# One parametric relu in place of a scaling and a bitwise and in the weights' split, with a new order of the program

## The chip, the cores and the metric

One NeuronCore of a Trainium2 chip runs the kernel. The metric is the device time of one execution in microseconds; three timed runs of the kernel before are shown.

## The reference

Windowed attention over 4 batches of 8 heads (768 positions, 64 values a head), then a feed-forward layer with a softmax-weighted activation on its output, seen as 3072 rows of 512:

```python
# _attn_ref, q, k, v of (4, 8, 768, 64); block 32, window 16
k_sum = k.reshape(B, H, nb, block, D).max(axis=3)
v_sum = v.reshape(B, H, nb, block, D).mean(axis=3)
scores_l = scale * q @ k^T          # kept where |i - j| < 16
scores_s = scale * q @ k_sum^T + log(block)
a = softmax(concat(scores_l masked, scores_s))
attn = a @ concat(v, v_sum)
# _moe_ref, x of (3072, 512), w_in 512 x 1024, w_out 1024 x 512
h = x @ w_in
solu = h * softmax(h)
ln = (solu - mean(solu)) / sqrt(var(solu) + 1e-6) * g_ln
return ln @ w_out
```

q, k, v and g_ln are float32 in memory; w_in and w_out come in as 64-bit floats and are cut into two 32-bit words each.

## The kernel before

The 3072 rows are 24 tiles of 128 rows. For each half of a group of 256 positions (a step, named by batch, group and half as 2_1_0) TensorE computes scores (tile s), VectorE their row maxima (L678), ScalarE the exponentials (L686), VectorE or GpSimd the division by the sum (tile e, L370 on VectorE or L371 on GpSimd), TensorE turns the result (tile t), ScalarE or VectorE copies it out of PSUM (tile at) and TensorE multiplies it by the values (tile x). Then, for each row tile, TensorE computes the first product (tile h; from row tile 8 on for two tiles at a time with seven instead of eight products: hu, hl, hf), the activation runs over ScalarE, VectorE and GpSimd (tile he), he is turned (by TensorE as lt, or from row tile 6 on by VectorE and a way through DRAM) and TensorE computes the second product (tile o), which ScalarE or VectorE scales (os) and a DMA writes out. Each product of 32-bit values is three matmuls: every operand is split into a high and a low part (xh and xl, lh and ll, two halves of w).

The weights arrive as pairs of words (tile raw, the high word in words(1), the low word in words(0)) in 16 pieces of 128 x 512: 8 of w_in (raw_97 to raw_103, raw_108 and raw_109), 8 of w_out (raw_124 to raw_131). `rounded` makes 32-bit floats of each in the tile cv: the high word scaled by 2^-112 (L454 on ScalarE or L456 on VectorE), its sign bit alone (L460, VectorE), the top of the low word (L465 or L467), a shift of the high word by three bits (L470), and the sum of the halves (ADD_W, L370 or L371). Then w's high part is a cast (w_in) or a scaling by g_ln (w_out, L487), and its low part a difference (w_out: L489). The centring of he stands in L1011 and its neighbours, the copies out of PSUM in L363 (ScalarE) and L364 (VectorE), the smaller of hm's two parts in L992.

Nothing is issued in the order in which it is written. Every step is an `op` with an engine, a duration that the planner assumes, the buffers that it reads and writes, and in places other engines with their durations. `Plan.order` lists the operations by these durations; `SEARCHED` is a list of seeds whose random shifts of due times and preferences were kept by a search. The result is one fixed instruction order on each engine. Into TensorE's order `issue` puts dummy matmuls on a zero tile (`idle`, L1300; 80 of them here) wherever the plan has TensorE waiting within its first 80 us. They write to a PSUM tile that is free and belong to no result.

Of the kernel before, what the change touches and what calls it, by code (L numbers as in the profile page):

```python
# [1345 lines left out]
```

## Time and profile before

| | us |
|---|---|
| median of three runs (lowest to highest) | 363.81 (363.76 to 363.94) |
| span of the profiled execution, first to last instruction | 362.6 |
| TensorE busy | 354.2 (98%) |
| VectorE busy | 305.5 (84%) |
| ScalarE busy | 281.6 (78%) |
| GpSimd busy | 157.3 (43%) |

The profiled execution has only its span; the runs' median is 1.2 us longer, which is the time that lies around the first and last instruction. Busy shares are averages over parts with different limits, and the ends of matmuls are modelled: a matmul of 512 columns is shown as some 0.39 us long although the next one starts 0.23 us later, so a wait of TensorE shows as idle only for the part that goes beyond that.

### The profile page before, as it was taken

The numbers are of one execution on the slowest core, as the hardware profiler recorded it, in microseconds if no ns is written. First come the engines' busy times: TensorE is split into PE (matmuls) and PEld (weight loads), VectorE is DVE, ScalarE is ACT, GpSimd is POOL, SyncE is SP. The second block draws the span as 40 slices with busy tenths as digits, with TensorE's granted clock in tenths as the row PEclk, the third lists the DMA queues.
The fourth block names the chain that finished last, engine by engine and source line by source line (L and its number), as shares of the span: only waits on it lengthen the run. The fifth ranks groups of instructions, "written<-read, shape, count | busy, mean of one in ns | idle before, by whom it ended". The sixth has DMA issues, their size and how long they took to land.

```text
span 362.6 us, 9384 instructions
## 1 busy us (share of the span) xinstructions
PE 354.2 (98%) x3332; PEld 277.0 (76%) x3332; DVE 305.5 (84%) x964; ACT 281.6 (78%) x815; POOL 157.3 (43%) x290
## 2 busy tenths in 40 slices
PE   8999999999999998999999999999999999999995
PEld 3537667768777786788788888888888888888885
DVE  4989999998999999997899999797797996947430
ACT  4888999979869978989698696896796796946320
POOL 6612330166968867423924147350335054534200
PEclk9999999999999999999999999999999999999999
DMA  7999994145325435538489384384164283344611
GB/s 241 413 414 405 359 397 155 62 113 165 130 77 196 136 131 173 172 95 273 141 270 285 117 280 153 114 288 148 57 201 174 55 276 101 116 147 168 209 58 58
DMA packets 28530, 68.19 MB, mean 188 GB/s; under 512 B 3852, under 2 KB 13324, under 8 KB 26948
## 3 DMA queue, kind: packets, MB, share of 16 engines
q1 hardware_dynamic: 24620, 60.87, 49.6%
q10 hardware_dynamic: 3864, 6.74, 5.2%
q8 instruction: 26, 0.43, 0.5%
q14 instruction: 20, 0.16, 0.1%
HBM read 49.55 MB, written 15.73 MB: 180 GB/s over the span
## 4 chain that ended last, share of the span: by engine, by line
PE 63%; DVE 22%; DMA 5%; ACT 3%; SPq 3%; issue 2%; POOL 1%; ACTq 0%; DVEq 0%
PE o L1108 29%; PE hu L932 10%; PE hl L932 5%; PE x L761 4%; PE s L659 3%; PE h L913 3%; DVE e L678 3%; PE t L714 3%; DMA qt<-in_q 2%; DMA farl<-tbl 2%; PE hf L932 2%; DVE e L370 2%; SPq L602 2%; DVE w L489 2%; DVE hm L990 2%
## 5 line engine op out<-in xcount | busy, mean ns | idle before, releaser
L1108 PE MATMUL o<-w,lh 128*128 128x512 f32 (+1 forms) x400 | 128.0, 385 | 0.9 <-DVE w L489 0.9
L1108 PEld LDWEIGHTS o<-w,lh 128*128 128x128 f32 x400 | 74.1, 188 | 16.4 <-DVE w L489 1.2
L1108 PE MATMUL o<-w,ll 128*128 128x512 f32 (+1 forms) x200 | 76.2, 381 | 0.0
L686 ACT ACTIVATE e<-e,nm 128x120 f32<-128x120 f32 x192 | 73.2, 388 | 0.0
L913 PE MATMUL h<-w,xh 128*128 128x512 f32 x128 | 43.0, 400 | 0.0
L1108 PEld LDWEIGHTS o<-w,ll 128*128 128x128 f32 x200 | 37.6, 188 | 6.8
L678 DVE CUSTOM_DVE_ANT_0 e<-s,mask 128x120 f32<-128x120 f32 x192 | 40.6, 276 | 0.5 <-PE s L659 0.3
L686 ACT ACTIVATION_READ_ACCUMULATOR e<-e,nm 128x1 f32 x192 | 37.0, 193 | 0.0
L363 ACT COPY at<-t 120x512 f32<-120x512 f32 x43 | 22.9, 591 | 11.0 <-PE t L714 8.6
L913 PEld LDWEIGHTS h<-w,xh 128*128 128x128 f32 x128 | 24.0, 188 | 7.3 <-ACT at L363 0.8
L1015 ACT ACTIVATE he<-he,nmu 128x512 f32<-128x512 f32 x36 | 24.7, 721 | 4.4 <-DVE nmu L1006 4.3
L761 PEld LDWEIGHTS x<-at,vt 120*64 120x64 f32 (+1 forms) x768 | 24.4, 138 | 4.1 <-issue 2.6
L371 POOL TENSOR_TENSOR ll<-lt,lh 128x512 fp32r<-128x512 f32 x11 | 16.5, 1512 | 23.5 <-DVE lh L364 15.8
L1038 DVE STREAM_TRANSPOSE tbl<-he 128x1024 f32<-128x1024 f32 x18 | 22.3, 1239 | 5.3 <-DMA farl<-tbl 2.7
L1114 ACT ACTIVATE os<-o,y 128x512 f32<-128x512 f32 (+1 forms) x20 | 13.5, 675 | 17.0 <-PE o L1108 16.8
L761 PE MATMUL x<-at,vt 120*64 120x64 f32 (+1 forms) x768 | 26.5, 224 | 0.0
L588 POOL TENSOR_TENSOR st_v<-st_v 96x512 f32<-96x512 f32 (+3 forms) x28 | 22.1, 797 | 8.3 <-DMA st_v<-in_vb 7.8
L1018 ACT ACTIVATE sq<-he 128x1024 bf16<-128x1024 f32 x24 | 25.3, 1056 | 0.1
L913 PE MATMUL h<-w,xl 128*128 128x512 f32 x64 | 25.1, 393 | 0.3 <-DVE xl L770 0.3
L363 ACT CAST lh<-lt 128x512 fp32r<-128x512 f32 x33 | 19.2, 608 | 7.8 <-DMA lt<-farl 5.6
L995 ACT ACTIVATE he<-hs,hm 128x512 f32<-128x512 f32 x24 | 17.1, 716 | 8.3 <-DVE hm L985 8.3
L370 DVE TENSOR_TENSOR e<-e,z 128x960 f32<-128x960 f32 x18 | 23.1, 1281 | 0.1
(175 smaller groups left out, 836.0 us busy)
## 6 DMA issues: line engine op xcount, KB each, us to landing
vt<-in_v SPq DMA_DIRECT2D x12, 1024.0 KB
farl<-tbl SPq DMA_DIRECT2D x18, 512.0 KB
lt<-farl SPq DMA_DIRECT2D x72, 128.0 KB
kraw<-in_k SPq DMA_DIRECT2D x16, 400.0 KB
out<-os ACTq DMA_DIRECT2D x23, 256.0 KB
qt<-in_q SPq DMA_DIRECT2D x11, 512.0 KB
raw<-in_w_in SPq DMA_DIRECT2D x8, 512.0 KB
raw<-in_w_out SPq DMA_DIRECT2D x8, 512.0 KB
```

What stands on the lines that cost most here:

```text
L363: by = {act: lambda: nc.scalar.copy(out=to(), in_=of()), dve: lambda: nc.vector.tensor_copy(out=to(), in_=of()), pool: lambda: nc.gpsimd.t ...
L370: by = {dve: lambda: nc.vector.tensor_tensor(out=to(), in0=a(), in1=b(), op=kind), pool: lambda: nc.gpsimd.tensor_tensor(out=to(), in0=a() ...
L588: op(pool, 0.15 + w * 0.0021, lambda w=w, o=o: nc.gpsimd.tensor_tensor(out=o.ap[:n, :w], in0=x.ap[:n, :w], in1=x.ap[:n, w:2 * w], op=ALU.add),
L678: nc.vector.tensor_tensor_reduce(out=e.ap[:, n, :], in0=sc.ap[:, j, (2 * i + up) * KC:(2 * i + up + 1) * KC], in1=mask[:, mi, :], scale=-S ...
L686: nc.scalar.activation(out=e.ap[:, n, :], in_=e.ap[:, n, :], func=AF.Exp, bias=nm.ap[:, n:n + 1], scale=-1.0, accum_out=z.ap[:, n:n + 1])
L761: nc.tensor.matmul(xp()[j * D:(j + 1) * D, i, qs], vs.ap[:k, u, cs], at.ap[:k, u % 2, n[j] + u // 2, :], start=not apart, stop=not apart o ...
L913: nc.tensor.matmul(hp.ap, a.ap[:, c, ts], w.ap[:, i], start=(c == 0 and n == 0), stop=(c == NKC - 1 and n == 2))
L932: nc.tensor.matmul(to.ap, operand(y, n)[:, c], w(c).ap(i), start=first and c == 0 and k == 0, stop=c == 1 and k == 2, skip_group_check=True)
L1015: (act, 0.57, lambda sl=sl: nc.scalar.activation(out=e.ap[:, sl], in_=e.ap[:, sl], func=AF.Identity, bias=nmu.ap))], port=True)
L1018: op(act, 1.13, lambda: nc.scalar.activation(out=sq.ap, in_=e.ap, func=AF.Square, accum_out=ss.ap), r=[e], w=[sq, ss])
L1038: op(dve, 1.13, lambda: nc.vector.transpose(out=tb.ap.rearrange("p (q c a) -> p q c a", q=4, a=32), in_=of().rearrange("p (c q a) -> p q c ...
L1108: nc.tensor.matmul(o.ap[:, cols], a.ap[:, f, :], w.ap[:, i, cols], start=(f == 0 and n == 0), stop=(f == NFC - 1 and n == 2))
```

## The change

In `rounded` the scaling of the high word becomes a parametric relu of ScalarE (Prelu). For a positive word it multiplies by 2^-112 as before; for a negative one by 2^-112 and by alpha = -2^32, so that the result is positive with an exponent that is 32 larger, and the shift by three bits that follows turns just that into the sign bit. The bitwise and (L460 of before) goes, and the low word is written as a whole 32-bit word instead of into the lower half of the word that held the sign. VectorE is no longer a choice for the scaling; it stays one for the low word.

The durations that the planner assumes are set to new values, corrections of some of TensorE's (`off`) go, and the list of seeds is a new one, so the order of all five engines is new. The list of first loads is unchanged.

```diff
-    SEARCHED = -856134719, -860457018, 52477149, 195803496, 905169564, -371301522, -289478668, -495083861, -295360282,\
+    SEARCHED = -749593861, -777804421, -802396418, -589041268, -104509395, -553513320, -224063771, -992918941,\
...
-    COPY_KS = ((pool, 0.35), (dve, 0.19))
+    COPY_KS = ((pool, 0.305), (dve, 0.19))
...
-    COPY_X = ((act, 0.48), (dve, 0.6))
+    COPY_X = ((act, 0.473), (dve, 0.6))
...
-    ADD_W = ((dve, 0.6), (pool, 1.3))
-    MUL_E = ((pool, 1.8), (dve, 1.07))
+    ADD_W = ((dve, 0.6), (pool, 1.23))
+    MUL_E = ((pool, 1.75), (dve, 1.07))
...
         op(act, 0.57, lambda: nc.scalar.activation(
-            out=high().bitcast(F32), in_=words(1).bitcast(F32), func=AF.Copy, scale=2.0 ** -112),
-            r=[x], w=[(st, 0)], alt=[(dve, 0.34, lambda: nc.vector.tensor_scalar(
-                out=high().bitcast(F32), in0=words(1).bitcast(F32), scalar1=2.0 ** -112, scalar2=None,
-                op0=ALU.mult))], port=True)
-
-        op(dve, 0.34, lambda: nc.vector.tensor_scalar(
-            out=low(), in0=words(1), scalar1=-2 ** 31, scalar2=None, op0=ALU.bitwise_and),
-            r=[x], w=[(st, 1)], port=True)
-
-        units = lambda: low().bitcast(U16).rearrange("p (n t) -> p n t", t=2)[:, :, 0]
-        op(act, 0.6, lambda: nc.scalar.activation(
-            out=units(), in_=words(0).bitcast(U32), func=AF.Copy, scale=2.0 ** -29), r=[x], w=[(st, 1)],
+            out=high().bitcast(F32), in_=words(1).bitcast(F32), func=AF.Prelu, scale=2.0 ** -112, alpha=-2.0 ** 32),
+            r=[x], w=[(st, 0)], port=True)
+
+        op(act, 0.65, lambda: nc.scalar.activation(
+            out=low(), in_=words(0).bitcast(U32), func=AF.Copy, scale=2.0 ** -29), r=[x], w=[(st, 1)],
             alt=[(dve, 0.34, lambda: nc.vector.tensor_scalar(
-                out=units(), in0=words(0).bitcast(U32), scalar1=2.0 ** -29, scalar2=None, op0=ALU.mult))], port=True)
+                out=low(), in0=words(0).bitcast(U32), scalar1=2.0 ** -29, scalar2=None, op0=ALU.mult))], port=True)
...
-            op(pe, 0.695, mm, r=[(hi, c), (lo, c), w], w=[hp])
+            op(pe, 0.68, mm, r=[(hi, c), (lo, c), w], w=[hp])
...
-            parts = [run(scores(*step(t + i)), off=0.18) for i in (4, 5) if t + 4 < NT]
-            parts += [run(values(*step(t + i)), off=0.23 - 0.05 * (i - 2)) for i in (2, 3)]
+            parts = [run(scores(*step(t + i))) for i in (4, 5) if t + 4 < NT]
+            parts += [run(values(*step(t + i))) for i in (2, 3)]
```

Counted over the whole program: the 16 bitwise ands go. The scaling stands 12 times on ScalarE and 4 times on VectorE before, 16 times on ScalarE after; the low word 8 and 8 times before, 6 and 10 after; the sum of the halves 11 times on VectorE and 5 on GpSimd before, 10 and 6 after. Of the 24 divisions (e) GpSimd has 6 before and 8 after; of the 48 centrings of he ScalarE, VectorE and GpSimd have 36, 3 and 9 before, and 26, 6 and 16 after. The dummy matmuls are 80 before and 82 after; before the means of the values (tile vs_ps, L546) stand 62 and 57 of them, behind it 18 and 25. All other matmuls are the same in number. The table of ScalarE's functions is loaded once, at the start, in both.

VectorE at the last two of the eight pieces of w_out (raw_130 and raw_131; the lines of after are 7 smaller from the cut on), of before:

```order
L460 TENSOR_SCALAR cv_1125<-raw_130 128x512
L470 TENSOR_SCALAR cv_1125<-cv_1125 128x512
L467 TENSOR_SCALAR cv_1125<-raw_130 128x512
L460 TENSOR_SCALAR cv_1144<-raw_131 128x512
L370 ISA cv_1125<-cv_1125 128x1024
L526 TENSOR_REDUCE ksum_0_165<-kraw_0_159 128x24
L470 TENSOR_SCALAR cv_1144<-cv_1144 128x512
L526 TENSOR_REDUCE ksum_0_165<-kraw_0_159 128x24
L489 SCALAR_TENSOR_TENSOR w_1157<-cv_1125,g_sb,w_1157 128x512
L692 RECIPROCAL z_2_1_1097<-z_2_1_1097 128x8
L770 TENSOR_TENSOR xl_2_1185<-x_2_0_1070,xh_2_1166 128x512
L489 SCALAR_TENSOR_TENSOR w_1179<-cv_1144,g_sb,w_1179 128x512
```

and the same place of after (L463 is now the shift, L482 the difference):

```order
L519 TENSOR_REDUCE ksum_0_165<-kraw_0_159 128x24
L983 TENSOR_REDUCE hm_179<-h_1_1074 128x1
L463 TENSOR_SCALAR cv_1117<-cv_1117 128x512
L685 RECIPROCAL z_2_1_1031<-z_2_1_1031 128x8
L983 TENSOR_REDUCE hm_179<-h_0_991 128x1
L370 TENSOR_TENSOR e_2_1_998<-e_2_1_998,z_2_1_1031 128x960
L482 SCALAR_TENSOR_TENSOR w_1151<-cv_1080,g_sb,w_1151 128x512
L763 TENSOR_TENSOR xl_2_1167<-x_2_0_1037,xh_2_1141 128x512
L370 ISA cv_1117<-cv_1117 128x1024
L364 COPY kw_0_0_1149<-kraw_0_159 128x8x96
L1079 TENSOR_TENSOR ll_1188<-lt_1123,lh_1176 128x8x64 x2
L482 SCALAR_TENSOR_TENSOR w_1186<-cv_1117,g_sb,w_1186 128x512
```

The two ands are gone, the low word stands ahead of this piece, and the division of e_2_1 stands on VectorE here (before it was GpSimd's).

TensorE at step 2_0 of batch 0 (the zero rows are dummy matmuls, each with a load of the zero weights that is left out here), of before:

```order
L714 MATMUL t_2_0_1032<-ident,e_2_0_937 120x64 x16
L1300 MATMUL x_2_0_1070<-zero 128x512
L761 MATMUL x_2_0_1070<-at_2_0_1066,vt_2_681 64x64 x16
L714 MATMUL lt_1102<-ident,he_856 128x64 x16
L913 MATMUL h_1_1121<-w_306,xh_1_135 128x512
```

and of after:

```order
L1293 MATMUL x_2_0_1037<-zero 128x512
L707 MATMUL t_2_0_1043<-ident,e_2_0_927 120x64 x16
L1293 MATMUL x_2_0_1037<-zero 128x512
L906 MATMUL h_1_1074<-w_344,xh_1_135 128x512
L754 MATMUL x_2_0_1037<-at_2_0_1063,vt_2_673 64x64 x16
L707 MATMUL lt_1123<-ident,he_842 128x64 x16
```

Before, six dummies stand behind t_2_0; after, five stand ahead of it and seven behind it, and the twelve matmuls of h_1 come ahead of x_2_0 instead of behind lt (of rows that repeat, one stands here).

TensorE at the first product of row tile 0, of before:

```order
L913 MATMUL h_0_498<-w_226,xh_0_117 128x512
L913 MATMUL h_0_498<-w_351,xh_0_117 128x512
L913 MATMUL h_0_498<-w_445,xh_0_117 128x512
L913 MATMUL h_0_498<-w_574,xh_0_117 128x512
L913 MATMUL h_1_636<-w_306,xh_0_117 128x512
```

and of after:

```order
L906 MATMUL h_1_587<-w_344,xh_0_117 128x512
L906 MATMUL h_0_484<-w_285,xh_0_117 128x512
L906 MATMUL h_0_484<-w_224,xh_0_117 128x512
L906 MATMUL h_1_587<-w_424,xh_0_117 128x512
L906 MATMUL h_0_484<-w_478,xh_0_117 128x512
```

Each row here is the first of three matmuls with one piece of weights; pieces 0 and 1 (w_226 and w_306 before, w_285 and w_344 after) and 2 and 3 (w_351 and w_450, w_224 and w_424) go with the half of x that is ready first. Before, two such threes come ahead of the first that needs the second half of x; after, four.

## Rows read from the trace of the kernel before

**Rows 1.** The page's head and its first part: the span, and for each engine its busy time, the share of the span and the number of instructions.
```profile
span 362.6 us, 9384 instructions
...
PE 354.2 (98%) x3332; PEld 277.0 (76%) x3332; DVE 305.5 (84%) x964; ACT 281.6 (78%) x815; POOL 157.3 (43%) x290
```

**Rows 2.** Busy time of each engine in stretches of the span: the stretch (us) and its length; then PE, PEld, DVE, ACT, POOL, SP with busy us and instructions in brackets; then granted TensorE clock as a share of full speed, the share of the DMA engines, GB/s.
```profile
40.00:50.00 10.00, 9.95 (x89) 6.14 (x89) 9.93 (x38) 10.00 (x31) 3.08 (x2) 1.00 1.02 412
...
60.00:80.00 20.00, 19.11 (x205) 14.24 (x204) 19.99 (x54) 17.49 (x46) 6.06 (x7) 1.00 0.28 78
...
180.00:200.00 20.00, 20.00 (x226) 16.86 (x225) 19.55 (x70) 18.49 (x60) 7.68 (x18) 1.00 0.86 263
```

**Rows 3.** The chain that ended last, in order of time (start, us, engine, operation): its long last piece.
```profile
325.93 32.96 PE o L1108 x168
```

**Rows 4.** TensorE in order of time (start, us, line, operation, tile, count, in brackets the idle time before it and who ended it): pairs of neighbouring rows.
```profile
95.18 1.15 PE L761 MATMUL x<-at,vt 120*64 120x64 f32 x32
96.27 0.50 PE L913 MATMUL h<-w,xh 128*128 128x512 f32 x1
...
117.72 0.39 PE L1108 MATMUL o<-w,lh 128*128 128x512 f32 x1
118.04 0.68 PE L714 MATMUL t<-ident,e 64*120 64x64 f32 x16
...
33.37 0.79 PE L913 MATMUL h<-w,xh 128*128 128x512 f32 x2
34.42 0.50 PE L913 MATMUL h<-w,xl 128*128 128x512 f32 x1 [0.26 <-DVE xl L770]
...
75.35 0.39 PE L1300 MATMUL x<-zero 128*128 128x512 bf16 x1
76.63 0.50 PE L1108 MATMUL o<-w,lh 128*128 128x512 f32 x1 [0.89 <-DVE w L489]
...
123.42 1.15 PE L761 MATMUL x<-at,vt 120*64 120x64 f32 x32
124.90 1.05 PE L659 MATMUL s<-kw,qt 64*64 64x120 f32 x32 [0.32 <-issue]
...
136.66 0.39 PE L1108 MATMUL o<-w,lh 128*128 128x512 f32 x1
137.55 0.68 PE L714 MATMUL t<-ident,e 64*120 64x64 f32 x16 [0.50 <-POOL e L371]
...
138.66 1.15 PE L761 MATMUL x<-at,vt 120*64 120x64 f32 x32
140.70 1.05 PE L659 MATMUL s<-kw,qt 64*64 64x120 f32 x32 [0.89 <-ACT at L363]
...
173.44 1.48 PE L714 MATMUL t<-ident,e 64*120 64x64 f32 x32
174.86 0.50 PE L932 MATMUL hu<-ws,xh 128*128 128x512 f32 x1
```

**Rows 5.** VectorE and GpSimd (POOL) in order of time at two places, then three of the groups by line (busy us, mean ns of one | idle time before them and what ended it).
```profile
74.24 1.79 POOL L371 TENSOR_TENSOR e<-e,z 128x960 f32<-128x960 f32 x1
74.63 1.94 DVE L489 SCALAR_TENSOR_TENSOR w<-cv,g_sb,w 128x512 fp32r<-128x512 f32 x1
...
135.37 2.13 POOL L371 TENSOR_TENSOR e<-e,z 128x960 f32<-128x960 f32 x1 [0.66 <-DVE z L692]
135.77 1.74 DVE L992 TENSOR_TENSOR hm<-hm 128x1 f32<-128x1 f32 x1
...
L992 DVE TENSOR_TENSOR hm<-hm 128x1 f32<-128x1 f32 x8 | 3.2, 394 | 0.0
L370 DVE TENSOR_TENSOR e<-e,z 128x960 f32<-128x960 f32 x18 | 23.1, 1281 | 0.1
L371 POOL TENSOR_TENSOR e<-e,z 128x960 f32<-128x960 f32 x6 | 11.1, 1848 | 8.5 <-DVE z L692 7.7 <-DVE hm L992 0.7
```

**Rows 6.** Instructions of the weights' split (tile cv): line, engine, operation, count, shortest/median/longest duration in ns, first and last start, shapes.
```profile
L460 DVE TENSOR_SCALAR cv<-raw x16: 411/428/1511, 4.7 to 69.8; 128x512 int32<-128x512 int32 x16
L454 ACT ACTIVATE cv<-raw x12: 646/674/682, 4.7 to 70.5; 128x512 f32<-128x512 f32 x12
L370 DVE CUSTOM_DVE_ANT_0 cv<-cv x11: 682/684/694, 6.1 to 70.1; 128x1024 uint16<-128x1024 uint16 x11
L465 ACT ACTIVATE cv<-raw x8: 763/780/796, 5.3 to 71.1; 128x512 uint16<-128x512 uint32 x8
L467 DVE TENSOR_SCALAR cv<-raw x8: 442/456/471, 18.9 to 69.5; 128x512 uint16<-128x512 uint32 x8
L489 DVE SCALAR_TENSOR_TENSOR w<-cv,g_sb,w x8: 741/749/1944, 39.6 to 74.6; 128x512 fp32r<-128x512 f32 x8
```

**Rows 7.** TensorE in order of time, columns as in group 4: dummy matmuls (L1300) and what follows one run of them.
```profile
15.28 4.92 PE L1300 MATMUL vs_ps<-zero 128*128 128x512 bf16 x22
20.13 2.33 PE L546 MATMUL vs_ps<-st_v,sel 128*24 128x512 f32 x5
...
43.17 1.47 PE L1300 MATMUL x<-zero 128*128 128x512 bf16 x6
44.62 0.50 PE L913 MATMUL h<-w,xh 128*128 128x512 f32 x1
```

**Rows 8.** ScalarE's last instruction, in order of time.
```profile
358.97 0.47 ACT L1114 ACTIVATE os<-o,y 128x256 f32<-128x256 f32 x1 [5.06 <-PE o L1108]
```

More of the change, by code (lines that the diff above doesn't have):

```diff
@@ L571, in mean_values_pe @@
         for g in range(4):
-            op(act, 0.34, lambda g=g: nc.scalar.dma_start(
+            op(act, 0.55, lambda g=g: nc.scalar.dma_start(
                 out=y.ap[WIN + 6 * g:WIN + 6 * g + 6, :], in_=rows.ap[32 * g:32 * g + 6, :]),
@@ L690, in scores @@
             op(act, 1.52, lambda i=i: exps(i), r=[nm], w=[(e, i), (z, i)])
-        op(act, 0.2, lambda: nc.scalar.activation(out=z.ap, in_=z.ap, func=AF.Copy, bias=1e-9), w=[z])
-        op(dve, 0.1, lambda: nc.vector.reciprocal(out=z.ap, in_=z.ap), w=[z])
+        op(act, 0.11, lambda: nc.scalar.activation(out=z.ap, in_=z.ap, func=AF.Copy, bias=1e-9), w=[z])
+        op(dve, 0.08, lambda: nc.vector.reciprocal(out=z.ap, in_=z.ap), w=[z])
         tt(MUL_E, ALU.mult, lambda: e.ap, lambda: e.ap,
@@ L695, in scores, with run @@
         es[b, g, pp] = e
-    def run(*parts, rest=True, off=0.0):
+    def run(*parts, rest=True):
         mine = [x for x in ((f, next(f, None)) for f in parts) if x[1]]
@@ L701, in run @@
             cost, fns, r, w = zip(*(x for _, x in mine))
-            op(pe, sum(cost) - 0.25 * (len(mine) - 1) - off, lambda: [f() for f in fns],
+            op(pe, sum(cost), lambda: [f() for f in fns],
                r=[x for y in r for x in y], w=[x for y in w for x in y])
@@ L763, in mm @@
                             start=not apart, stop=not apart or u == G - 1, skip_group_check=apart)
-        yield 2.2 if apart else 1.17, mm, [vs, at] + [vm] * apart, [xb]
+        yield 1.9 if apart else 1.03, mm, [vs, at] + [vm] * apart, [xb]
         if NG * b + g >= FAST:
@@ L802, in wide @@
                 "p (k i c) -> p k i c", k=m, i=2)
-        half, whole = ((act, 0.34), (dve, 0.33)), ((act, 0.48), (dve, 0.6))
+        half, whole = ((act, 0.26), (dve, 0.33)), ((act, 0.473), (dve, 0.6))
         lo_h, lo_w = [(dve, 0.33)], [(dve, 0.6)]
@@ L811, in combine @@
                r=[xb, (f, 0)], w=[(f, 1)])
-            split(hi, lo, 1, 1, 0, lambda: of(1), [(f, 1)], (((act, 0.34), (dve, 0.2)), lo_hs))
+            split(hi, lo, 1, 1, 0, lambda: of(1), [(f, 1)], (((act, 0.3), (dve, 0.2)), lo_hs))
         else:
@@ L821, in combine @@
             split(hi2, lo2, 0, 2, 0, lambda: of(0, 2), [(f, 0), (f, 1)], (((act, 0.55), (dve, 0.34)), lo_ws))
-            split(hi2, lo2, 2, 1, 0, lambda: of(2), [(f, 2)], (((act, 0.34), (dve, 0.2)), lo_hs))
+            split(hi2, lo2, 2, 1, 0, lambda: of(2), [(f, 2)], (((act, 0.3), (dve, 0.2)), lo_hs))
     class Sub:
@@ L994, in solu @@
         for i, (hp, key) in enumerate(hs):
-            op(act, 0.71, lambda i=i, hp=hp: nc.scalar.activation(
+            op(act, 0.68, lambda i=i, hp=hp: nc.scalar.activation(
                 out=part(i), in_=hp(), func=AF.Exp, bias=nm.ap, accum_out=zs.ap[:, i:i + 1]),
@@ L1000, in solu @@
            w=[zs])
-        op(dve, 0.1, lambda: nc.vector.reciprocal(out=zs.ap[:, 0:1], in_=zs.ap[:, 0:1]), w=[zs])
+        op(dve, 0.07, lambda: nc.vector.reciprocal(out=zs.ap[:, 0:1], in_=zs.ap[:, 0:1]), w=[zs])
         for i, (hp, key) in enumerate(hs):
@@ L1014, in solu @@
                 out=e.ap[:, sl], in0=e.ap[:, sl], scalar1=nmu.ap, scalar2=None, op0=ALU.add)),
-                (act, 0.57, lambda sl=sl: nc.scalar.activation(
+                (act, 0.615, lambda sl=sl: nc.scalar.activation(
                     out=e.ap[:, sl], in_=e.ap[:, sl], func=AF.Identity, bias=nmu.ap))], port=True)
         sq = plan.buf(sb, [P, DF], BF16, "sq", 1, f"sq{t}")
-        op(act, 1.13, lambda: nc.scalar.activation(
+        op(act, 1.04, lambda: nc.scalar.activation(
             out=sq.ap, in_=e.ap, func=AF.Square, accum_out=ss.ap), r=[e], w=[sq, ss])
-        mul = lambda to, x: op(pool, 0.3, lambda: nc.gpsimd.tensor_tensor(out=to.ap, in0=to.ap, in1=x.ap, op=ALU.mult), r=[x], w=[to])
+        mul = lambda to, x: op(pool, 0.26, lambda: nc.gpsimd.tensor_tensor(out=to.ap, in0=to.ap, in1=x.ap, op=ALU.mult), r=[x], w=[to])
         op(pool, 0.3, lambda: nc.gpsimd.tensor_scalar(
             out=ss.ap, in0=ss.ap, scalar1=1.0 / DF, scalar2=1e-6, op0=ALU.mult, op1=ALU.add), w=[ss])
-        op(pool, 0.46, lambda: nc.gpsimd.tensor_tensor(out=y.ap, in0=ss.ap, in1=mhalf, op=ALU.pow),
+        op(pool, 0.52, lambda: nc.gpsimd.tensor_tensor(out=y.ap, in0=ss.ap, in1=mhalf, op=ALU.pow),
            r=[ss], w=[y])
@@ L1027, in solu @@
         mul(ss, y)
-        op(pool, 0.3, lambda: nc.gpsimd.tensor_scalar(
+        op(pool, 0.15, lambda: nc.gpsimd.tensor_scalar(
             out=ss.ap, in0=ss.ap, scalar1=-0.5, scalar2=1.5, op0=ALU.mult, op1=ALU.add), w=[ss])
@@ L1037, in send @@
         tb = plan.buf(sb, [P, DF], F32, "tb", 1, f"tb{name}")
-        op(dve, 1.13, lambda: nc.vector.transpose(
+        op(dve, 1.16, lambda: nc.vector.transpose(
             out=tb.ap.rearrange("p (q c a) -> p q c a", q=4, a=32),
@@ L1067, in rows_split @@
             of = lambda r=r: lt.ap.rearrange("p i (c a) -> p c i a", a=32)[:, 4 * r:4 * r + 4]
-            copy(((act, 0.48), (dve, 0.34)), lambda part=part: part(hi), of, r=[lt], w=[(hi, r)], port=True)
+            copy(((act, 0.508), (dve, 0.335)), lambda part=part: part(hi), of, r=[lt], w=[(hi, r)], port=True)
             tt(LO_W, ALU.subtract, lambda part=part: part(lo), of, lambda part=part: part(hi).bitcast(F32),
@@ L1110, in mm @@
                             stop=(f == NFC - 1 and n == 2))
-                op(pe, 0.695 * k, mm, r=[hi, lo, wt[2 * NKC + f]], w=[o])
+                op(pe, 0.04 + 0.64 * k, mm, r=[hi, lo, wt[2 * NKC + f]], w=[o])
                 yield
             os = plan.buf(sb, [P, DM], F32, "os", 2, f"os{t}")
-            op(act, 0.1 + 0.46 * k, lambda o=o, os=os, cols=cols: nc.scalar.activation(
+            op(act, 0.14 + 0.446 * k, lambda o=o, os=os, cols=cols: nc.scalar.activation(
                 out=os.ap[:, cols], in_=o.ap[:, cols], func=AF.Copy, scale=y.ap),
@@ L1117, in second_parts @@
                    out=os.ap[:, cols], in0=o.ap[:, cols], scalar1=y.ap, scalar2=None, op0=ALU.mult))])
-            op(act, 0.34, lambda os=os, cols=cols: nc.scalar.dma_start(
+            op(act, 0.45, lambda os=os, cols=cols: nc.scalar.dma_start(
                 out=out[t * P:(t + 1) * P, cols], in_=os.ap[:, cols]), r=[os], nbytes=int(P * 2048 * k))
@@ L1257, in turns @@
             steps = [i for i in (t + 2, t + 3) if i < NT and i != PAIRED + 2]
-            chain([run(values_turn(*step(i)), off=0.1 if i < steps[-1] else 0.0) for i in steps])
+            chain([run(values_turn(*step(i))) for i in steps])
         behind = second_parts(t - 4 - (t > LATER))
@@ L1281, in attn_then_solu @@
             second(t - 3)
-            chain([run(turn(t - 2), off=0.09), run(turn(t - 1), off=0.14)])
+            chain([run(turn(t - 2)), run(turn(t - 1))])
         if 0 < b < B - 1 and g < 2:
```

10 lines of the change are left out of this document (5 added, 5 removed), and 22 rows, old and new, of the table SEARCHED.

## The prediction

> **What bounds the kernel now.** I read the page's first part, then the busy time by stretches, then TensorE in order of time. Over the whole span TensorE is busy 98% and VectorE 84% [rows 1], which sounds like a TensorE kernel with nothing to gain but TensorE work. The stretches say that the kernel has two parts. From 180 us on TensorE is busy 20.00 of 20 us [rows 2], and the chain ends with one unbroken piece of matmuls, 325.93 + 32.96 = 358.89 us [rows 3]; after it come only the last scaling, 358.97 + 0.47 [rows 8], and its DMA. In that part every other engine runs ahead of TensorE, so nothing that the change saves there can move the end, and the end moves by just as much as TensorE reaches 180 us earlier or later. Before that, VectorE is the full engine: 9.93 of 10 us at 40 to 50, where ScalarE has 10.00, and 19.99 of 20 at 60 to 80, while TensorE has 19.11 [rows 2].
>
> So the question is how much TensorE waits before 180 us. The idle time in brackets hides part of it, because the modelled end of a matmul lies behind the start of the next. I therefore take distances from start to start and subtract the usual one. Usual are 96.27 − 95.18 = 1.09 us from a step's x to the next group, and 118.04 − 117.72 = 0.32 from a last o to a t [rows 4]; a matmul of 512 columns takes 0.24, by six dummies in 44.62 − 43.17 = 1.45 us [rows 7]. The long distances, all in [rows 4]:
> - 33.37 to 34.42: 1.05 for two matmuls, 0.57 too long (second half of xl from VectorE);
> - 75.35 to 76.63: 1.28 for one, 1.04 too long (w's low part, L489 on VectorE);
> - 123.42 to 124.90: 1.48, 0.39 too long (behind x; no releaser shown);
> - 136.66 to 137.55: 0.89, 0.57 too long (division of e on GpSimd, L371);
> - 138.66 to 140.70: 2.04, 0.95 too long (ScalarE's copies of at);
> - 173.44 to 174.86: 1.42, 0.34 too long.
>
> The sum is 3.86 us. That is all that a better order or a lighter VectorE can win behind the first scores; the rest of the span is matmuls. The start is a further wait: 22 dummies at 15.28 fill the time until vs_ps at 20.13 [rows 7]. It hangs on the first loads, whose list stays the same, and I count it as unchanged.
>
> **The change, part by part.** *VectorE's share of the split.* From [rows 6]: 16 ands at 0.428 go, −6.85 us; four scalings go to ScalarE, −1.7 at the and's price (same form, one scalar operation); two low words come, 2 × 0.456 = +0.9; one sum goes to GpSimd, −0.68. Together −8.3 us, all between 4.7 and 75 us, on the engine that is full there. *ScalarE's share.* Four scalings come, 4 × 0.674 = +2.7, and two low words go, −2 × 0.780 = −1.6; the six that stay now write whole words and may cost what the scaling costs, six times 0.1 less. So +0.5 to +1.1 us; ScalarE had 17.49 of 20 us at 60 to 80 [rows 2], where this fits, and none left at 40 to 50. What Prelu costs no row shows. Below, it is the scaling's 0.674 (the same words in and out, one pass); above, twice that, if a second pass were needed, 16 × 0.674 = +10.8 us. I take 0.674, the row nearest in form.
>
> *What VectorE's relief is worth.* TensorE takes it only where VectorE made it wait. Four of the waits are VectorE's, at first hand or at second: xl at 34.42, where the twelve matmuls that now stand ahead of xl, not six, add 6 × 0.24 = 1.4 us of cover; w at 76.63; at behind 138.66; and the division at 137.55. The middle two have one history [rows 5]. At 74.63 L489 took 1.94 us while GpSimd divided e from 74.24 to 76.03; its usual time is 0.749 [rows 6]. At 135.77 a minute L992 took 1.74 us, its eight together 3.2, so the seven others some 0.2 each, again under a division on GpSimd (135.37, 2.13 us instead of the mean 1.85). Each time VectorE stood still for 1.2 to 1.5 us until GpSimd was through, and TensorE's wait came right behind. In the new order the division of e_2_1 beside the last weights stands on VectorE (1.28 us there), so the first is gone with its cause, and VectorE is 8.3 us lighter by then. The Trainium skill states the mechanism (SBUF — State Buffer, Who interferes with whom): VectorE and GpSimd share one pair of ports, whoever starts first holds it for the whole instruction, and the other blocks; the two rows agree, with 1.94 and 1.74 us. By that rule the change would be judged by the divisions that it gives to GpSimd, and that speaks against it: it gives the 365.6 us of the second rival, where the sum without it gives the forecast.
>
> I take 3.9 us of waits gone and 0.7 us new or left. The new order will have some: in it the copies of at for two steps stand behind a cast or an os on ScalarE, and the waits at 123.42 and 173.44, 0.39 + 0.34 = 0.7 us, have no VectorE cause, which is the size that I keep. Ends: 0 left, and all 3.9 left.
>
> *Dummies and order on TensorE.* All result matmuls stay. Behind vs_ps there are 25 dummies instead of 18: 7 × 0.24 = 1.7 us that TensorE executes in its own order. Where it would have waited anyway they cost nothing; where the relief ends the wait, they cost their time. Lower end 0, upper end 1.7; since VectorE is to be ahead, I take 1.7. The dummies ahead of vs_ps, 57 instead of 62, lie in the wait for the first loads, and that wait covers them.
>
> *Other engines.* GpSimd gets two divisions more at 1.85 us [rows 5], seven centrings and one sum; at 157.3 us of 362.6 [rows 1] it has the room, and what it costs is only the ports. In the part from 180 us on the centrings leave ScalarE lighter, which is hidden behind TensorE. SP's and POOL's queues issue their later loads in another sequence. I cost that at nothing: at 60 to 80 us VectorE has no idle time in which it could have waited for a piece (19.99 of 20), so the split is what comes late, not the load. Were a piece late after all, TensorE would wait as it did for w at 76.63, some 1 us.
>
> **The sum.** The profiled execution has a span of 362.6 us [rows 1], the median of the runs is 363.81; the 1.2 between them lies outside the span and stays. 362.6 − 3.9 + 0.7 + 1.7 = 361.1 us of span, and 361.1 + 1.2 = 362.3 us, 1.5 us or 0.4% less.
>
> **Rivals.** *Waits that only move (same).* VectorE's 8.3 us are gained before 80 us, but each tile still hangs on the chain exponentials, division, turning, copy, product, with ScalarE full at 40 to 50 and heavier now. If half or more of the waits come back in other places (1.6 to 3.0 us left), the time is 363.81 − 3.9 + 1.7 + 2.3 = 363.9 at the middle. For it: two of the six waits name neither VectorE nor a division. Against it: the largest does.
>
> *GpSimd's larger share (slower).* Eight divisions instead of six, 16 centrings instead of 9. Each division on GpSimd can hold TensorE itself for 0.57 us (as at 137.55) or hold VectorE for 1.2 to 1.5 us and TensorE behind it for 1.0. If four of the eight do so, at 0.57 to 1.0, 2.3 to 4.0 us are left and more with one at copy late, 1.0: up to 5. It decides from 2.9 us on, since −3.9 + 1.7 + 2.9 = +0.7. At 4.0 us left the time is 365.6. Against it: of the six divisions before, two did so, and VectorE had no slack then.
>
> *The change doesn't do what it says.* If Prelu takes two passes, ScalarE gets 10.8 us more in its full stretch and becomes the engine that TensorE waits for; even a third of that on the path gives 362.3 + 3.6 = 365.9. Against it: the scaling needs one pass, and slope and scale are both factors that it applies to each element anyway.
>
> **How the numbers follow.** The forecast (0.2 to 1.5 us left) gives 361.8 to 363.1 us and has 0.63; it holds because the causes of the two largest waits are taken away in the order itself. Waits that only move have 0.20, GpSimd's share 0.13, Prelu 0.04. A measurement of this kernel can tell some 0.2%, 0.73 us, so faster is below 363.08, slower above 364.54. A little of the forecast's upper end is "same", and a little of the lower end of the moved waits is "faster"; that gives faster 0.63, same 0.21, slower 0.16. The range begins 0.7 + 0.4 below the forecast (no wait left, and dummies that are partly free): 361.2. Upward it takes in the moved waits, to 364.3; above it lie the slower cases, some 0.17, and below it some 0.03. The forecast's own range is 361.8 to 363.1.
>
> **What would show it.** Right: the split has no and, 16 Prelu at about 0.67 us on ScalarE, VectorE below 19 of 20 us at 60 to 80; no wait for w at the last pieces of w_out; TensorE gapless from 175 us on as before, with its last piece starting 1 to 2 us earlier; vs_ps where it was, at 20.1. Wrong: a difference of w (L482 there) or a minute operation on VectorE of over 1.5 us under a division on GpSimd, with a wait of TensorE behind; Prelu over 0.8 us; first scores later than before, which no term holds.

## The result and the profile after

The changed kernel takes 367.6 us (367.05 to 369.44) where the kernel before takes 363.88 in the same runs: 3.7 us more, a ratio of 1.0109 with a 95% interval of 1.0094 to 1.0124. The prediction was 362.3 in a range of 361.2 to 364.3.

The first profile is of the slowest execution, 369.44 us. A second one, of the unchanged kernel once more (a_again, below), is of one of 368.36, the slowest of its four, with a span of 366.1 and TensorE at full clock; numbers below are from it where nothing else is said.

The page of the changed kernel, first profile, its head and first part (as [rows 1]):

```profile
span 367.7 us, 9379 instructions
...
PE 356.4 (97%) x3334; PEld 277.2 (75%) x3334; DVE 293.7 (80%) x940; ACT 276.7 (75%) x814; POOL 162.8 (44%) x299
```

VectorE is 11.8 us lighter (8.3 were reckoned for the split), and the span is longer all the same. The split's instructions, second profile (as [rows 6]):

```profile
L454 ACT ACTIVATE cv<-raw x16: 645/670/702, 5.8 to 70.2; 128x512 f32<-128x512 f32 x16
...
L460 DVE TENSOR_SCALAR cv<-raw x10: 415/418/435, 5.8 to 67.9; 128x512 int32<-128x512 uint32 x10
```

L454 is Prelu now: 0.670 us, what the plain scaling took (0.674 in [rows 6]). The low word in one whole word takes 0.418 instead of 0.456. So the split itself came out as reckoned. Busy time by stretches, second profile (columns as in [rows 2]):

```profile
60.00:80.00 20.00, 20.00 (x209) 14.48 (x207) 19.37 (x56) 16.65 (x47) 5.19 (x7) 1.00 0.21 62
160.00:180.00 20.00, 19.11 (x113) 15.00 (x117) 19.17 (x48) 16.12 (x54) 14.44 (x25) 1.00 0.74 225
180.00:200.00 20.00, 19.49 (x196) 15.67 (x194) 19.39 (x67) 19.43 (x62) 9.66 (x11) 1.00 0.83 270
```

At 60 to 80 us TensorE now has 20.00 instead of 19.11, so no wait shows there any more (a_seven below finds one of 1.0 us under dummies, which count as busy). But between 160 and 200 us it has 19.11 and 19.49, where the kernel before had its full 20.00 from 180 us on. That is one place. The other is the end. TensorE's last matmul and ScalarE's last instructions, second profile (time, us, engine; ACTq is the issue of a transfer):

```profile
359.55 0.39 PE L1101 MATMUL o<-w,lh 128*128 128x512 f32 x1
360.02 0.69 ACT L1107 ACTIVATE os<-o,y 128x512 f32<-128x512 f32 x1 [9.53 <-PE o L1101]
360.74 0.34 ACTq L1111 DMA_DIRECT2D out<-os  x1
361.18 0.47 ACT L1107 ACTIVATE os<-o,y 128x256 f32<-128x256 f32 x1 [0.47 <-ACT os L1107]
361.68 0.34 ACTq L1111 DMA_DIRECT2D out<-os  x1
362.79 0.47 ACT L1107 ACTIVATE os<-o,y 128x256 f32<-128x256 f32 x1 [1.13 <-DMA out<-os]
363.29 0.34 ACTq L1111 DMA_DIRECT2D out<-os  x1
```

Before, one scaling of 256 columns followed the last matmul ([rows 8]), and behind it two transfers were issued in a row:

```profile
359.47 0.82 ACTq L1118 DMA_DIRECT2D out<-os  x2
```

From that matmul's start (358.60 in that trace) to the span's end it took 4.00 us. Now three scalings follow on one engine, and the third waits 1.13 us for a transfer, because os has two buffers and the first still holds a tile that is being written out: 366.1 − 359.55 = 6.55 us. The order of after shows it without any trace. TensorE's last six rows of after are three matmuls each of (one of the three stands here):

```order
L1101 MATMUL o_5080<-w_1186,lh_5031 128x256
L1101 MATMUL o_5024<-w_1186,lh_4989 128x512
```

o_5024 is row tile 22, o_5080 the second half of row tile 23: one piece of tile 22 was left behind 23's sixteen, and so tile 22 is ready last. The second profile accounts for the 3.5 us between the spans (362.6 and 366.1) by three stretches. Start: the means of the values begin at 20.62 instead of 20.13, +0.5 (no more than single executions differ by: 19.90 to 20.52 in the six profiles with the order of before or an edit of it). Middle, from there to the last matmul's start: 338.93 instead of 338.47, +0.5. End: 6.55 instead of 4.00, +2.5.

### The profile page after: what moved, and what is told of

Its sections match the earlier page's. It is cut to its first block, busy times and chain, and to the rows that moved or that the text cites. A ratio compares the mean times of both kernels' runs of the same rounds, so it can differ in the third digit from the quotient of the medians.

```text
span 367.7 us, 9379 instructions
## 1 busy us (share of the span) xinstructions
PE 356.4 (97%) x3334; PEld 277.2 (75%) x3334; DVE 293.7 (80%) x940; ACT 276.7 (75%) x814; POOL 162.8 (44%) x299
## 4 chain that ended last, share of the span: by engine, by line
PE 82%; ACT 6%; DMA 4%; POOL 4%; DVE 3%; issue 1%; POOLq 0%; ACTq 0%
PE o L1101 31%; PE h L906 11%; PE hu L925 10%; PE x L754 6%; PE hl L925 6%; PE s L652 6%; PE t L707 3%; PE hf L925 3%; PE vs_ps L1293 2%; DMA st_v<-in_vb 2%; ACT e L679 2%; PE vs_ps L539 1%; DMA raw<-in_w_in 1%; PE x L1293 1%; POOL st_v L581 1%; ACT at L363 1%
## 5 line engine op out<-in xcount | busy, mean ns | idle before, releaser
L363 ACT CAST lh<-lt 128x512 fp32r<-128x512 f32 x39 | 22.8, 611 | 19.4 <-PE o L1101 13.4
L363 ACT COPY at<-t 120x512 f32<-120x512 f32 x40 | 21.6, 588 | 16.0 <-PE t L707 7.9
L370 DVE TENSOR_TENSOR ll<-lt,lh 128x512 fp32r<-128x512 f32 x25 | 22.2, 902 | 11.4 <-ACT lh L363 11.4
L1004 POOL TENSOR_SCALAR he<-he,nmu 128x512 f32<-128x512 f32 x16 | 11.1, 696 | 32.2 <-DVE nmu L999 25.7
L1107 ACT ACTIVATE os<-o,y 128x512 f32<-128x512 f32 (+1 forms) x19 | 12.6, 662 | 16.7 <-PE o L1101 14.6
L581 POOL TENSOR_TENSOR st_v<-st_v 96x512 f32<-96x512 f32 (+3 forms) x28 | 22.9, 832 | 5.0 <-DMA st_v<-in_vb 4.3
L371 POOL TENSOR_TENSOR ll<-lt,lh 128x512 fp32r<-128x512 f32 x11 | 14.3, 1309 | 23.0 <-DVE lh L364 8.8
L365 POOL COPY kw<-ksum 128x192 f32<-128x192 f32 x21 | 8.4, 406 | 32.2 <-PE s L652 25.2
```

The source lines that it names most:

```text
L363: by = {act: lambda: nc.scalar.copy(out=to(), in_=of()), dve: lambda: nc.vector.tensor_copy(out=to(), in_=of()), pool: lambda: nc.gpsimd.t ...
L370: by = {dve: lambda: nc.vector.tensor_tensor(out=to(), in0=a(), in1=b(), op=kind), pool: lambda: nc.gpsimd.tensor_tensor(out=to(), in0=a() ...
L581: op(pool, 0.15 + w * 0.0021, lambda w=w, o=o: nc.gpsimd.tensor_tensor(out=o.ap[:n, :w], in0=x.ap[:n, :w], in1=x.ap[:n, w:2 * w], op=ALU.add),
```

## The experiments

All were timed in three rounds beside the kernel before, and each is given as its ratio to it (1.0109 for the changed kernel). 0.001 is 0.36 us.

| kernel | median us | ratio, 95% interval |
|---|---|---|
| a_tail: after, end mended | 364.44 | 1.0018 (1.0009 to 1.0027) |
| a_again: after, unchanged | 367.42 | 1.0088 (1.0063 to 1.0113) |
| a_start: after, 9 dummies more | 368.29 | 1.0127 (1.0112 to 1.0142) |
| a_both: both | 365.06 | 1.0032 (1.0022 to 1.0042) |
| b_short: before, 9 dummies fewer | 364.38 | 1.0015 (1.0004 to 1.0025) |
| b_tail: before with after's end | 366.42 | 1.0076 (1.0061 to 1.0091) |
| a_div: a_tail, one division moved | 363.50 | 0.9992 (0.9979 to 1.0004) |
| a_div2: a_div, a difference moved too | 363.84 | 1.0008 (0.9997 to 1.0019) |
| a_seven: a_tail, 7 dummies fewer | 364.06 | 1.0006 (0.9994 to 1.0018) |
| a_and: a_tail, ands put back | 366.66 | 1.0085 (1.0060 to 1.0109) |
| b_split: before, the split alone | 363.44 | 0.9984 (0.9974 to 0.9994) |
| b_div: before, two divisions moved | 362.87 | 0.9972 (0.9961 to 0.9984) |
| b_split_div: both of these | 362.64 | 0.9972 (0.9958 to 0.9985) |

### The end: a_tail and b_tail

```diff
+        last = next(o for o in order if tag(o) == "o22_0_7")
+        order.remove(last)
+        order.insert(next(i for i, o in enumerate(order) if tag(o).startswith("o23_")), last)
```

> The changed kernel with one thing moved: the last piece (three matmuls) of row tile 22's second product stands ahead of row tile 23's instead of behind it. Theory: the end of the changed kernel is longer because row tile 22 becomes ready last, so that three scalings queue up on ScalarE and the third waits 1.1 us for a buffer whose transfer has just begun; 6.6 us from the last matmul's start to the span's end against 4.0 before. Moved, this is 4.0 again: 2.5 us less than the changed kernel, 365.0 us. Rival: the end hangs on the output transfers' queue whatever the order, and the time stays at 367.5.

It fell to 364.44, 3.2 us below the changed kernel. Its last matmul and ScalarE's last rows:

```profile
358.84 0.28 PE L1105 MATMUL o<-w,lh 128*128 128x256 f32 x1
...
359.16 0.47 ACT L1111 ACTIVATE os<-o,y 128x256 f32<-128x256 f32 x1 [2.35 <-PE o L1105]
359.66 0.34 ACTq L1115 DMA_DIRECT2D out<-os  x1
```

One scaling and one transfer follow the last matmul, and with a span of 362.4 the end is 3.6 us long, shorter than the 4.00 of before with its two transfers. From the means of the values to the last matmul it is 338.93 us in both profiles, so the edit changed the end alone.

```diff
+        ends = {getattr(o, "tag", ""): o for o in order}
+        ends = [ends[x] for x in ("o22_0_7", "os22_0", "out22_0", "os23_0", "out23_0", "os23_256", "out23_256")]
+        for o in ends:
+            o.engine, (o.cost, o.fn) = o.first, o.can[o.first]
+        order = [o for o in order if o not in ends] + ends
```

> The kernel before with the changed kernel's end: the last three matmuls of row tile 22's second product stand behind row tile 23's, and the three last scalings follow one another on ScalarE, with their transfers; nothing else. Theory: the end costs what it cost in the changed kernel, 3 us: 367.0. Rival: that end was only long because other transfers were late there: 363.8 to 364.5.

The same end put onto the kernel before costs 2.6 us by the medians. Its last matmul starts at 358.67, where it was before, and the span is 365.2: 6.5 us of end. Taken away in one kernel and put into the other, the end order is worth 2.6 to 3.2 us by the medians (2.5 and 3.0 by the ends in the profiles). It is by far the largest part of the result, and it has nothing to do with the new split.

### The start: a_start, a_both, b_short, a_again

The first profile had made me look for a third cause. Windows of it (the stretch and its length, then PE, PEld, DVE, ACT, POOL, then the granted clock, the DMA share and GB/s):

```profile
8.00:10.00 2.00, 0.44 (x3) 0.19 (x2) 1.44 (x2) 1.66 (x3) 0.00 (x0) 1.00 1.03 335
10.00:12.00 2.00, 1.83 (x33) 1.12 (x34) 1.97 (x5) 1.57 (x3) 0.00 (x0) 0.73 1.01 399
12.00:14.00 2.00, 2.00 (x35) 1.25 (x34) 2.00 (x5) 0.96 (x2) 0.93 (x2) 0.50 1.05 423
```

The new order has 25 dummies ahead of the first scores, not 34. TensorE is busy for 0.44 of 2 us at 8 to 10, then works at half clock (1.2 GHz) at 12 to 14, and the means of the values start at 21.68.

```diff
+                for _ in range(9 * (not any(x.engine == "pe" for x in done))):
+                    self.keep_up(at, done)
```

> The changed kernel with nine more dummy matmuls ahead of the first scores (34 as before, not 25). Theory: with 25, TensorE stands still twice (0.9 and 0.8 us) ahead of and in the first scores, its granted clock then falls to 1.2 GHz from about 11 to 15.5 us, and everything behind comes 1.5 us later. With 34 there is no wait, the clock stays, the means of the values start at 20.1 as in the kernel before: 1.5 us less than the changed kernel, 366.0. Rival: the start hangs on the first loads and on VectorE's sums; then the means of the values start at 21.7 all the same and the time stays at 367.5.

> Both edits at once. If both theories hold and the two places are independent, 4.0 us less than the changed kernel: 363.5 us, within 0.2% of the kernel before (363.9), because in between the waits that the change takes away are paid back by dummies and new waits. If the start's gain is eaten by a wait behind it, 365.

> The kernel before with nine dummy matmuls fewer ahead of the first scores (25 instead of 34), nothing else. Theory of the clock: TensorE stands still for about 2 us ahead of the first scores, its clock falls, and the time goes up by about 1.5 us to 365.4. Rival (the start hangs on loads alone): 363.9, no change.

 (Its edit leaves out the first nine calls of idle.)

> The changed kernel once more, unchanged, for a second profile. In the first, which was its slowest execution (369.44 us beside 367.05 to 367.62), TensorE's clock fell at 10.9 us and the means of the values started at 21.7. If the fall belongs to single executions only, the new profile has full clock at 10 to 16 us, the means at 19.8 to 20.8, the last matmul at 359 to 360, a span of 365 to 366 and the same 6 us behind it; the median stays at 367.5. If it belongs to the kernel, the means start at 21.7 again.

The theory fell. Nine dummies more made the kernel no faster: 368.29 beside 367.6, and 365.06 beside 364.44 where the end was mended, so by the medians they cost some 0.6 us, with intervals that overlap. The means of the values start at 20.54 and 20.78 with 34 dummies, no earlier than in the full-clock profiles with 25 (19.91 to 20.79). Nine fewer cost the kernel before 0.5 us (0.1 to 0.9), not 1.5. The second profile of the unchanged kernel shows the standstill without the fall:

```profile
8.00:10.00 2.00, 0.66 (x5) 0.20 (x4) 1.61 (x3) 1.78 (x4) 0.00 (x0) 1.00 1.04 381
10.00:12.00 2.00, 2.00 (x41) 1.25 (x43) 1.97 (x4) 1.43 (x3) 0.07 (x1) 1.00 1.01 401
12.00:14.00 2.00, 2.00 (x37) 1.10 (x36) 2.00 (x4) 1.12 (x2) 1.03 (x2) 1.00 1.05 419
```

TensorE stands still there nearly as long, and the clock stays full. So the fall belongs to that one execution. Of the fourteen profiles taken since the change it is the only one with it. Its means of the values start 1.1 us later than in the second profile (21.68 beside 20.62); that all of this comes from the clock is not shown. What decides whether the clock falls stays open.

### The middle: a_div, a_div2, a_seven

With the end mended the changed order is still 0.7 us slower than before, where the sum had promised 1.5 us less. TensorE's waits of the second profile (engine, tile, what it waited for, us, times, longest):

```profile
PE s L652 <- DVE ksum L519: 0.9, 1, 0.9
PE hu L925 <- DVE hx L935: 0.8, 1, 0.8
PE s L652 <- DMA qt<-in_q: 0.5, 1, 0.5
PE x L754 <- DVE at L364: 0.4, 1, 0.4
PE hf L925 <- ACT he L1008: 0.4, 1, 0.4
PE x L746 <- ACT at L363: 0.2, 1, 0.2
```

The two for s are those of the start. By distances, as in the prediction, the others are 0.98 (hu at 176.89), 0.50, 0.57 (hf at 190.88) and 0.27 (x at 28.36). Two more show by distance alone: a hu at 189.50 comes 0.27 late, and a step's t at 173.74 is 0.28 too long. Together they are 2.9 us. Only the last stands where one stood before (173.44). The largest has this history, on GpSimd and VectorE in the second profile, in order of time:

```profile
166.26 5.74 POOL L581 TENSOR_TENSOR st_v<-st_v 96x512 f32<-96x512 f32 x5 [3.00 <-DMA st_v<-in_vb]
171.95 0.74 POOL L371 TENSOR_TENSOR xl<-sums,xh 128x256 fp32r<-128x256 f32 x1
172.06 4.17 DVE L370 TENSOR_TENSOR ll<-lt,lh 128x512 fp32r<-128x512 f32 x1
172.64 1.80 POOL L371 TENSOR_TENSOR e<-e,z 128x960 f32<-128x960 f32 x1
174.39 1.28 POOL L371 TENSOR_TENSOR ll<-lt,lh 128x512 fp32r<-128x512 f32 x1
176.15 0.68 DVE L935 CUSTOM_DVE_ANT_0 hs<-hu,hs 128x512 f32<-128x512 f32 x1
```

VectorE's ll, usually some 0.7 us, takes 4.17 (5.07 in the first profile). It ends 0.56 us after GpSimd's own ll, three instructions of GpSimd later: here it did not come in between them. Behind it hs is late, and TensorE's hu behind hs. This looks like the mechanism of [rows 5], with some 3.5 us of hold where I had priced 1.2 to 1.5. The Trainium skill (SBUF — State Buffer, Who interferes with whom) states the exclusive hold for one instruction; that VectorE stayed out through three GpSimd instructions in a row is what this trace adds. It is no rule, for in the kernel before VectorE's ll did come in between, behind a division on GpSimd (298.56 to 300.35):

```profile
299.23 1.68 DVE L370 TENSOR_TENSOR ll<-lt,lh 128x512 fp32r<-128x512 f32 x1
300.31 1.74 POOL L371 TENSOR_TENSOR ll<-lt,lh 128x512 fp32r<-128x512 f32 x1
```

VectorE's ll ends at 300.91, and it is GpSimd's ll that takes longer, 1.74 instead of 1.28. What decides between the two stays open.

```diff
+        for o in order:
+            if getattr(o, "tag", "") in ('e2_0_1',):
+                o.engine, (o.cost, o.fn) = "dve", o.can["dve"]
```

> The tail-mended changed kernel (the last piece of row tile 22's second product ahead of row tile 23's; 364.4 us) with one division of e taken from GpSimd to VectorE, that of batch 2, group 0, second half, which GpSimd executes at 174.2 us between its additions of st_v and a difference. Theory: GpSimd's row of two-input work from 168 to 177 us held VectorE for 5.07 us at 172.67, and TensorE's waits at 176.0, 178.4 and 192.4 (0.47, 0.98 and 0.57 us) come from it; without the division it is 1.0 to 2.0 us faster, 362.4 to 363.4. Rival: the additions of st_v alone hold VectorE as long, and the division's 1.15 us on VectorE itself takes the place: 364.4, or slower.

From 1.0018 to 0.9992: some 0.9 us, just short of the 1.0 to 2.0 expected. The profiles account for 0.3 of it (338.93 and 338.66 from the means of the values to the last matmul); where the rest lies is not shown. The hold did not end, it was cut. VectorE, GpSimd and the new wait of TensorE in a_div:

```profile
170.82 2.10 DVE L377 TENSOR_TENSOR e<-e,z 128x960 f32<-128x960 f32 x1
...
171.86 1.64 POOL L378 TENSOR_TENSOR xl<-sums,xh 128x256 fp32r<-128x256 f32 x1
...
172.84 2.45 DVE L377 TENSOR_TENSOR ll<-lt,lh 128x512 fp32r<-128x512 f32 x1
...
173.55 0.50 PE L933 MATMUL hl<-w,xl 128*128 128x512 f32 x1 [0.72 <-POOL xl L378]
```

The division takes 2.10 us on VectorE, begun under the additions of st_v, and it comes in ahead of GpSimd's xl, which now takes 1.64 instead of 0.74. VectorE's ll takes 2.45, and TensorE waits for GpSimd's xl instead of for hx. The late hu and hf of 189.50 and 190.88 are still there, with 0.25 and 0.57 us: the theory had put that hf down to the hold, and it does not come from there.

```diff
+        x = [o for o in order[:at] if o.engine == "pool"][-1]
+        x.engine, (x.cost, x.fn) = "dve", x.can["dve"]
```

> The tail-mended changed kernel with the division of batch 2, group 0, second half on VectorE (0.45 us faster than the kernel before), and with the difference xl ahead of it on VectorE too, for which TensorE then waited 0.88 us at 173.5. Theory: the additions of st_v on GpSimd keep its queue late, and what is taken out of it comes early: 0.5 to 0.9 us faster again, 362.5 to 363.0. Rival: VectorE is held by the additions and the wait changes its name: 363.4.

It gave nothing more (1.0008, the intervals overlap); TensorE now waits for e on VectorE, at 175.11. The wait changed its name, as the rival had it, but the additions are not what held VectorE there: they end at 172.32, and the division runs from 172.76 for 2.30 us beside GpSimd's own ll (172.75, 1.29 us). No run took the additions away.

> The tail-mended changed kernel without the seven dummy matmuls behind t of step 2_0 of batch 0 (at 67.5 us, ahead of h_1 of row tile 1), which the kernel before does not have in that place. Theory: they are executed on the path, 7 x 0.24: 1.6 us faster, 362.8. Rival: what follows waits anyway for e or for copies of at, and the 1.6 us come back as waits: 364.4.

 (Its edit leaves out the calls of idle from the 75th to the 81st.)

1.0006 beside 1.0018, 0.4 us with intervals that overlap; not the 1.6 of the theory, though the intervals do not exclude a part of it. TensorE in a_seven where the dummies were:

```profile
65.72 0.69 PE L718 MATMUL t<-ident,e 64*120 64x64 f32 x16
67.36 0.50 PE L917 MATMUL h<-w,xh 128*128 128x512 f32 x1 [0.95 <-DVE he L1007]
```

The next h waits 1.0 us for VectorE to have read the bank that it writes to. So 1.0 of the 1.7 us of the seven dummies lay in a wait that they hid from the profile.

### What the new split is worth: a_and, b_split, b_div, b_split_div

```diff
+        def sign():
+            nc.vector.tensor_scalar(
+                out=low(), in0=words(1), scalar1=-2 ** 31, scalar2=None, op0=ALU.bitwise_and)
```

> The tail-mended changed kernel with the sixteen bitwise ands put back on VectorE, each ahead of its low word in whose place it writes (result and order of the rest unchanged): 6.9 us more of VectorE before 76 us. If VectorE's relief is what pays, VectorE is late again at the splits and TensorE waits 1 to 4 us more: 365.5 to 368. If the relief is slack in this order: 364.4 to 364.8.

1.0085 beside 1.0018, 2.4 us slower. New waits stand in the stretch before 80 us. TensorE's, in a_and:

```profile
PE s L660 <- DVE ll L1087: 0.7, 1, 0.7
...
PE t L715 <- POOL e L375: 0.3, 1, 0.3
```

So the relief is no slack in the new order: put back, the ands cost time. Within its first 80 us VectorE is busy 66.9 us (second profile) where it was 71.9 before: 5.1 us less, not 8.3, because this order gives it other work there. But the 2.4 us are not VectorE's load alone. Where ScalarE writes the low word it now waits for VectorE's and, four times and 5.3 us in all (longest 2.2), which it does not do in a_tail. Which of the two TensorE waits for was not separated.

```diff
-        op(dve, 0.34, lambda: nc.vector.tensor_scalar(
+        op(dve, 0.34, lambda: top.engine == dve and nc.vector.tensor_scalar(
             out=low(), in0=words(1), scalar1=-2 ** 31, scalar2=None, op0=ALU.bitwise_and),
```

(top is the scaling, Prelu where it stands on ScalarE.)

> The kernel before in its own order with the new split alone: Prelu for the twelve scalings that stand on ScalarE, their ands gone, the low word whole; the four scalings on VectorE stay as they were. VectorE has 12 x 0.43 = 5.1 us less, and nothing else moves. If VectorE's relief pays by itself, the waits for xl (0.6) and w (1.05) go, and perhaps those at 124 to 141 us: 362.0 to 363.2. If waits only move: 363.7.

0.9984, 0.6 us (0.2 to 0.9), between the two outcomes expected. In the old order nearly every wait stays. GpSimd and VectorE in b_split, where TensorE waits for w:

```profile
74.00 1.79 POOL L371 TENSOR_TENSOR e<-e,z 128x960 f32<-128x960 f32 x1
74.40 1.94 DVE L489 SCALAR_TENSOR_TENSOR w<-cv,g_sb,w 128x512 fp32r<-128x512 f32 x1
...
76.40 0.50 PE L1108 MATMUL o<-w,lh 128*128 128x512 f32 x1 [0.67 <-DVE w L489]
```

L489 has its 1.94 us as in [rows 5]: a lighter VectorE is held just as long.

> The kernel before with two divisions of e moved from GpSimd to VectorE, those that stood beside L489 at 74.24 us and beside L992 at 135.37 us; the split as before. Theory of the ports: the waits for w at 76.6 (1.05), for e at 137.5 (0.56) and for s at 140.7 (0.95) have these two divisions as their cause and go: 1 to 2.5 us faster, 361.3 to 362.8. Rival: VectorE is the full engine there, and 1.15 us more of it each time costs as much as the hold did: 363.8 or slower.

> The kernel before with both: the new split in its own order (0.5 us faster alone) and the two divisions on VectorE. If the split pays once the holds are gone, more than the sum of the two alone: 361.0 to 362.0. If VectorE's load was no cause, the sum of the two.

b_div moves the divisions by the same three lines as a_div, with the names e0_2_1 and e1_2_0. It is 1.0 us faster than the kernel before (0.6 to 1.4), with the old split. In b_div, VectorE's L489 (L492 there), then VectorE, ScalarE and TensorE at the former 140.70:

```profile
74.76 0.74 DVE L492 SCALAR_TENSOR_TENSOR w<-cv,g_sb,w 128x512 fp32r<-128x512 f32 x1
...
135.26 1.14 DVE L373 TENSOR_TENSOR e<-e,z 128x960 f32<-128x960 f32 x1
...
136.50 0.69 ACT L999 ACTIVATE he<-h,hm 128x512 f32<-128x512 f32 x1 [3.12 <-DVE hm L996]
...
137.66 1.15 PE L765 MATMUL x<-at,vt 120*64 120x64 f32 x32
139.71 1.05 PE L662 MATMUL s<-kw,qt 64*64 64x120 f32 x32 [0.89 <-issue]
```

L492 is back at 0.74, and the waits for w and for e are gone. The wait behind x is not: 2.05 us from x to s, as before. ScalarE's chain that ends with the copies of at still begins when it gets hm, as in the kernel before:

```profile
137.54 0.69 ACT L995 ACTIVATE he<-h,hm 128x512 f32<-128x512 f32 x1 [3.65 <-DVE hm L992]
```

L992's hold of 1.5 us is gone, but the division, 1.14 us on VectorE itself, now stands ahead of it. So the chain begins 1.0 us earlier (136.50 for 137.54), x comes 1.0 us earlier too (137.66 for 138.66), and the distance stays. Here the rival was right: the division costs VectorE nearly what the hold did.

With the split added (b_split_div) the ratio is the same 0.9972, neither of the two outcomes expected: the 0.6 us that the split gains alone do not show on top. From the means of the values to the last matmul it takes 336.77 us, b_div 336.72. Both are faster than the kernel before and than the changed kernel.

## Why the prediction was wrong

*The end* was the step that failed most. "In that part every other engine runs ahead of TensorE, so nothing that the change saves there can move the end" was said of savings, and then used as if the new order could not cost anything there either. I compared the orders at the places where TensorE waited before, all ahead of 180 us, and not at the end, where both orders differ in three matmuls. In the prediction's own account it is a term that is missing, of 2.6 to 3.2 us. The sentence does not hold for TensorE's waits either: two of the new ones, 0.27 and 0.57 us, stand at 189.50 and 190.88. Without the end the changed order still takes 364.44 us (a_tail) for the 362.3 forecast; those 2.1 us are about what the term of new waits lacks (2.9 for 0.7).

*Waits gone, 3.9 us*: right but for the last. Five of the six places have no wait in the new order; the sixth, 0.34, is there with 0.28. That they went for the causes named is shown only in the old order, for w and e (b_div), where the wait behind x did not shrink. *Waits new or left, 0.7 us*: mis-sized; 2.9 us by distances, and 1.0 more under dummies. It took the two waits without a VectorE cause for the measure of a new order's waits, which is no argument for their size. The case of waits that only move, with 1.6 to 3.0 us, had 0.20 and was the right one for the middle. *GpSimd's larger share*: the mechanism came, at one place. The rows of [rows 5] showed it, and I priced a hold by single divisions (1.2 to 1.5 us) where VectorE's ll took 3.5 us longer than usual under a row of GpSimd's instructions.

*Dummies, 1.7 us*: the size cannot be told from a_seven's median (0.4 us, not told from nothing). Its trace stands between the two ends that I gave: 1.0 us of the 1.7 would have been a wait anyway. *The start*, counted as unchanged: 0.5 us later in the second profile, and from 19.91 to 20.79 in the other full-clock profiles with this order, beside 19.90 to 20.52 with the order of before. Right within that.

*Prelu and the split*: right, 0.670 us for 0.674, one table load. VectorE at 60 to 80 us did not fall below 19 of 20 us (19.37), since the new order fills it with other work.

Summed again with what was measured, to the median before: 363.8 − 3.9 + 2.9 + 1.7 + 0.5 (start) + 2.6 to 3.2 (end) = 367.6 to 368.2, where 367.6 was measured. The middle alone is − 3.9 + 2.9 + 1.7 = +0.7, where the two profiles differ by 0.5. The loosest term is the start's 0.5, which is no more than executions differ by.

## What to carry to other kernels

When a search makes a new order of a whole program, compare the two orders first at the very end and ask what follows the last matmul: how many results, on how many engines, through how many buffers. A stretch in which an engine has no slack to win still has time to lose. And before an engine is made lighter, read its longest instructions: where a 0.75 us instruction takes 1.9 beside one on another engine, try moving the neighbour first: two moved divisions gave 1.0 us here, 5 us less work on that engine 0.6 us (the intervals overlap).
